# Dividing attention outputs by their row sums: normalizing after a transpose, or scaling in place with a spread copy of the reciprocals

## The chip, the core and the metric

The kernel is one program on one core of a Trainium2 chip. The core has TensorE (PE; PEld is its weight load), VectorE (DVE), ScalarE (ACT) and GpSimd (POOL), which compute, and SyncE (SP), which here only issues DMAs. Each of them works off its own instructions in a fixed order and waits at an instruction until what it needs is there; what stands behind waits too. [...] The metric is device time in microseconds (us) of one execution, lower is better.

## What is computed

Top-32 attention for 8 batches and 8 heads, 576 queries and keys, head size 64, and then a mixing layer for each batch on the 576 x 512 outputs `x`:

```
scores = q @ k.T / 8
mask = scores >= (32nd largest of the row)
attn = exp(where(mask, scores, -1e9) - rowmax)
attn = attn / (sum(attn) + 1e-9)
x = attn @ v                      # heads side by side: [batch, 576, 512]

theta = x @ w_theta
zr, zi = x * cos(theta), x * sin(theta)
u = x + w_tok_r @ zr + w_tok_i @ zi
out = u + relu(u @ w_ch)
```

The division by `sum(attn)` is linear, so the kernel does it late: `attn @ v` is computed from the raw exponentials, and each query's 64 outputs of a head are multiplied by one reciprocal afterwards. That multiplication is what is changed.

## The kernel before

**Attention.** A batch has four pairs of heads, and a pair five units: four of 128 queries for two heads, and one (j = 4) that holds the last 64 queries of both heads. A unit runs through `scores` (TensorE products, ScalarE copies half of them out), `fold` and `pick` (VectorE), `threshold` (VectorE: MAX8 and MATCH_REPLACE8, then a row on GpSimd that makes `lim`), `penalize` (ScalarE makes `pen`, GpSimd subtracts it, L304), `exponent` (ScalarE, which sums the row as it goes), `turn` (TensorE transposes to keys on partitions, ScalarE copies `at`), `mix_values` (TensorE) and `keep_values`, where ScalarE copies the result into the batch's `xt`: channels on partitions, 4 blocks of 128, and 576 queries along the row. `pipeline` interleaves these over neighbouring units: a unit's scores are written two units ahead, its exponentials one unit and its transposes two units behind. The next pair is loaded ahead (`raw`, L171), halved into `hi` (ScalarE, L189) and `raw` (GpSimd, L190), and copied into place by twelve DMAs (L202) ahead of its first scores. `raw`, `hi` and the units' `e` share nine buffers.

**Mixer.** When the last pair of a batch is kept, a generator `mixer` starts, and `advance` lets it take steps between the units that follow: ten steps in the first five units (`PLAN`), then one a unit. The batch's row sums lie with queries on partitions (`sums`), and `rinv` is their reciprocal there. In the first steps each of five blocks k of queries goes through a chain:

- four transposes of `xt` into PSUM, `px_s` (L533): queries on partitions;
- `normalize` (L434, VectorE): `px_s` times `rinv`, written to `xs`;
- `turn_back`: four transposes of `xs` into `px_t` (L449), which ScalarE copies over `xt` (L450);
- `angles` (L472, L475): `xt` times `w_theta` into `pth`;
- `fraction` (L486 ScalarE, L487 VectorE): the fractional part of the angle, into `z`.

Block 4 has 64 queries; outside the last batch its 512 channels are folded into two halves on 128 partitions. Then `trig` takes sines and cosines on ScalarE (L494 to L496) and multiplies them by `xs` on GpSimd (L497, L502). The sine needs another table than the exponential: all sines of a batch stand between two table loads, and no exponential can stand between them. Then come the token products `py` (L576), to which VectorE adds `xt` (L557), the channel products `po` (L601) and the output (L602, stored at L603).

**What sets the order.** The kernel is written as one long program. A scheduler orders each engine's instructions by priority (the place in the program, less or plus an offset: mixer steps are 100 ahead, its token and channel products 400 behind, so that these fill gaps) and by when it takes operands and buffers to be ready. Within an engine the order is then fixed. `ps_t` has two PSUM buffers for all transposes, `xs` and `z` one buffer each. The last batch (`split`) runs its products in three passes of halved numbers, with nothing of attention left beside it. A safe path that computes everything again stands behind an `If` that isn't taken.

Of the kernel before, what the change touches and what calls it, by code (L numbers as in the profile page):

```python
# [9 lines left out]
F32 = mybir.dt.float32  # L10
# [5 lines left out]
ALU = mybir.AluOpType  # L16
AX = mybir.AxisListType

P = 128
# [3 lines left out]
WEARLY = 3  # L23
AHEAD = 2
S_LATE = 0
PLAN = (2, 2, 2, 2, 2)
ORDER = "PTUFKSTVMXZ"
FOLDS = 3
M_TOK = 400
M_PE = 0  # L30
# [14 lines left out]
def topk_attention_phase_mixer(  # L45
# [11 lines left out]
    nc = tc.nc  # L57
    B, NPAIR, _, S = qT.shape
    DM = w_ch.shape[0]
    D = P // 2  # L60
    H = 2 * NPAIR
    HS = S // 2
    NJ = S // P
    REM = S - NJ * P
    NB = DM // P
    KB = 2 * NJ + 1
# [7 lines left out]
    wk2 = ctx.enter_context(tc.tile_pool(name="wk2", bufs=2))  # L74
    wk3 = ctx.enter_context(tc.tile_pool(name="wk3", bufs=3))
    one = ctx.enter_context(tc.tile_pool(name="one", bufs=1))
    ps_s = ctx.enter_context(tc.tile_pool(name="ps_s", bufs=2, space=bass.MemoryType.PSUM))
    ps_t = ctx.enter_context(tc.tile_pool(name="ps_t", bufs=2, space=bass.MemoryType.PSUM))
    ps_m = ctx.enter_context(tc.tile_pool(name="ps_m", bufs=2, space=bass.MemoryType.PSUM))

    ident = const.tile([P, P], F32, name="ident")
# [80 lines left out]
    def later(n):  # L162
        return tc.high_priority(offset=-n)
# [236 lines left out]
    def mixer(bt, split=False):  # L400
        bq, xt, sums, sums_rem = bt["bq"], bt["xt"], bt["sums"], bt["sums_rem"]
        nc.gpsimd.tensor_copy(sums[:REM, NJ, 0::2], sums_rem[0:D])
        nc.scalar.copy(sums[:REM, NJ, 1::2], sums_rem[D:P])
        rinv = wk2.tile([P, NJ + 1, H], F32, tag="rinv", name="rinv")
# [20 lines left out]
                return xs[:REM, NJ], z[:REM, 2 * NJ], last[0][:REM]  # L425
            return xs[:, NJ, :HD], last[0][:, :HD], last[0][:, HD:]

        def normalize(k, px):
            rows, parts = (P, 1) if k < NJ else (REM, folds)
            for a in range(parts):  # L430
                cols = slice(a * DM // parts, (a + 1) * DM // parts)
                out = xs[a * D : a * D + rows, k, : DM // parts]
                hs = slice(cols.start // D, cols.stop // D)
                nc.vector.tensor_tensor(  # L434
                    out.rearrange("p (h d) -> p h d", d=D),
                    px[:rows, cols].rearrange("p (h d) -> p h d", d=D),
                    rinv[:rows, k, hs].unsqueeze(2).to_broadcast([rows, hs.stop - hs.start, D]),
                    op=ALU.mult,
                )

        def turn_back(j):
            rows, parts = (P, 1) if j < NJ else (REM, folds)
            m = NB // parts
            for a in range(parts):
                sl = slice(a * D, a * D + rows)
                pt = ps_t.tile([P, NB, P], F32, tag="t", name="px_t")
                with later(M_PE):
                    for p in range(m):
                        nc.tensor.transpose(pt[:, p, :rows], xs[sl, j, p * P : p * P + P], ident[sl, sl])  # L449
                nc.scalar.copy(xt[:, a * m : a * m + m, j * P : j * P + rows], pt[:, :m, :rows])  # L450
                if split:
                    cs = slice(j * P, j * P + rows)
                    nc.scalar.copy(x_hi[:, a * m : a * m + m, cs], pt[:, :m, :rows])
                    for p in range(a * m, a * m + m, 2):
                        pp = slice(p, p + 2)
                        nc.vector.tensor_sub(x_lo[p // 2][:, :, cs], xt[:, pp, cs], x_hi[:, pp, cs].bitcast(F32))

        def angles(j):
            th[j] = ps_m.tile([P, 512], F32, tag="m", name="pth")
# [17 lines left out]
                            )  # L477

        def fraction(j):
            whole = wk2.tile([P, DM], F32, tag="whole", name="whole", bufs=1)  # L480
            if j == NJ:
                last[0] = whole
            _, zr, _ = spots(j)
            n = zr.shape[-1]
            m = zr.shape[0]
            nc.scalar.activation(whole[:m, :n], th[j][:m, :n], AF.Identity, bias=magic[:m])  # L486
            nc.vector.scalar_tensor_tensor(  # L487
                zr, whole[:m, :n], MAGIC, th[j][:m, :n], op0=ALU.subtract, op1=ALU.subtract
            )
# [28 lines left out]
        if split:  # L518
# [5 lines left out]
                z_hi.extend(flat[:, k] for k in range(flat.shape[1]))  # L524
            z_lo += two_blocks("kh", NJ, DM, "z_lo") + two_blocks("q2", NJ, DM, "z_lo")
            z_lo.append(wk2.tile([P, S], F32R, tag="lo1", name="z_lo")[:, :DM])
        for k in range(NJ + 4):
            if k <= NJ:
                rows = P if k < NJ else REM
                px = ps_t.tile([P, DM], F32, tag="t", name="px_s")  # L530
                with later(M_PE):
                    for p in range(NB):
                        nc.tensor.transpose(px[:rows, p * P : p * P + P], xt[:, p, k * P : k * P + rows], ident)  # L533
                normalize(k, px)
            if 0 <= k - 1 <= NJ:
                turn_back(k - 1)
            if 0 <= k - 3 <= NJ:
                fraction(k - 3)
            if 0 <= k - 2 <= NJ:
                angles(k - 2)  # L540
            if k < NJ + 4:
                yield
        yield
        trig(range(NJ + 1))
        yield
        late = None
# [34 lines left out]
        settle(*late)  # L581
        for m in range(NB):
            if not split:
                ot = wk2.tile([P, S], F32, tag="ot", name="ot", bufs=1)
            else:
                if m % 2 == 0:
                    ots = wk2.tile([P, 2, S], F32, tag="kh", name="ots")
                ot = ots[:, m % 2]
# [186 lines left out]
```

## Time and profile before

| | |
|---|---|
| time, median of 3 runs | 1308.51 us (1308.46 to 1309.14) |
| the profiled execution's own time | 1313.39 us |
| its span, first to last instruction | 1311.5 us |
| busy: PE, DVE, ACT, POOL | 89%, 90%, 77%, 50% of the span |
| mean granted clock of TensorE | 0.95 of full speed |

The span is one core's, so there is nothing to compare between cores. The profiled execution took 4.9 us more than the median; terms worked out from its rows are set against its own time and then taken off the median. A busy share is a mean over stretches with different limits, so the views by stretch and the chain of waits say more than the shares. Durations on GpSimd are rough, and a matmul's end is modelled.

### The profile page before, as it was taken

Reading aid. Unit: us, or ns where it says so; the run is one execution under the profiler, and the core shown is the slowest. Engines: PE = TensorE matmul, PEld = TensorE weight load, DVE = VectorE, ACT = ScalarE, POOL = GpSimd, SP = SyncE. Lnnn points to the kernel's source line nnn. Section 1 sums busy time; section 2 is a strip of 40 time slices with the busy share of each in tenths; the row PEclk is TensorE's granted clock in tenths of the full one; section 3 lists DMA queues with packets and bytes.
Section 4 is the critical chain, followed back from the end, with each engine's and each line's share of the span. In section 5 each row is a group of like instructions: output and inputs, shape, how many; then the busy total and the mean of one; then the engine's idle time right before and its main releaser. Section 6 shows DMA issues by size and latency. Waiting matters only on the chain.

```text
span 1311.5 us, 21746 instructions
## 1 busy us (share of the span) xinstructions
PE 1169.6 (89%) x6293; PEld 859.9 (66%) x6293; DVE 1181.1 (90%) x3993; ACT 1011.9 (77%) x2072; POOL 650.6 (50%) x768
## 2 busy tenths in 40 slices
PE   3666669899989998899999998899999999899998
PEld 3544445678657775577656785577756786567688
DVE  7999999899999999979999999889999999888453
ACT  4878778978788788977879878886888878786660
POOL 2445655744475445643465534553464544653640
PEclk9878769999989999999999999999998999999999
DMA  5234441433323333123323243123423144120001
GB/s 171 58 84 117 141 125 48 108 82 101 100 63 82 82 110 91 41 76 92 109 55 90 79 113 91 36 59 89 136 55 90 37 115 130 27 64 10 37 2 39
DMA packets 70720, 106.04 MB, mean 81 GB/s; under 512 B 13888, under 2 KB 32064, under 8 KB 70592
## 3 DMA queue, kind: packets, MB, share of 16 engines
q1 hardware_dynamic: 70592, 104.57, 29.5%
q8 instruction: 52, 0.85, 0.3%
q14 instruction: 76, 0.62, 0.2%
HBM read 38.40 MB, written 9.44 MB: 36 GB/s over the span
## 4 chain that ended last, share of the span: by engine, by line
PE 38%; DVE 32%; ACT 15%; issue 4%; POOL 4%; SPq 3%; DMA 3%; ACTq 0%; POOLq 0%; DVEq 0%
PE py L576 14%; DVE lst L283 9%; DVE lst L289 8%; PE pth L472 6%; PE px L357 5%; PE ps_score L234 4%; PE pt L329 3%; DVE lst L265 3%; DVE lo L266 3%; DVE lst L270 3%; SPq L202 3%; ACT e L314 3%; ACT pen L302 2%; PE po L601 2%; ACT e L243 2%
## 5 line engine op out<-in xcount | busy, mean ns | idle before, releaser
L304 POOL TENSOR_TENSOR e<-e,pen 128x576 f32<-128x576 f32 x288 | 369.1, 1299 | 208.4 <-ACT pen L302 195.4
L283 DVE MAX8 lst<-lst 128x8 f32<-128x192 f32 (+3 forms) x1152 | 423.9, 407 | 0.8
L289 DVE MATCH_REPLACE8 lst<-lst 128x192 f32<-128x192 f32 (+2 forms) x864 | 329.7, 388 | 0.0
L576 PE MATMUL py<-w,z 128*128 128x288 f32 x1008 | 272.0, 414 | 1.2 <-DMA z<-whole 1.2
L314 ACT ACTIVATE e<-e,lim 128x576 f32<-128x576 f32 x288 | 225.3, 784 | 36.4 <-POOL e L304 35.1
L234 PE MATMUL ps_score<-kh,q 128*128 128x288 f32 x512 | 188.9, 383 | 59.0 <-DVE lo L266 25.3
L302 ACT ACTIVATE pen<-e,lim 128x576 bf16<-128x576 f32 x288 | 210.7, 775 | 39.5 <-POOL lim L294 39.4
L576 PEld LDWEIGHTS py<-w,z 128*128 128x128 f32 x1008 | 185.7, 193 | 54.4 <-issue 7.1
L329 PE MATMUL pt<-ident,e 128*128 128x128 f32 x1152 | 178.6, 288 | 34.8 <-ACT e L314 21.1
L329 PEld LDWEIGHTS pt<-ident,e 128*128 128x128 f32 x1152 | 141.0, 146 | 76.4 <-ACT e L314 27.2
L357 PE MATMUL px<-at,vt 128*64 128x320 f32 (+1 forms) x1024 | 171.0, 430 | 7.7 <-ACT at L334 5.3
L243 ACT COPY e<-ps_score 128x576 f32<-128x576 f32 x256 | 162.0, 647 | 18.9 <-PE ps_score L234 14.7
L331 ACT COPY at<-pt 128x512 f32<-128x512 f32 x256 | 145.2, 587 | 28.0 <-PE pt L329 27.3
L234 PE MATMUL ps_score<-kl,q 128*128 128x288 f32 x512 | 157.5, 323 | 4.5 <-DMA kl<-raw 3.9
L234 PEld LDWEIGHTS ps_score<-kh,q 128*128 128x128 f32 x512 | 104.7, 205 | 81.9 <-ACT e L243 23.1
L265 DVE TENSOR_TENSOR lst<-ps_score,e 128x576 f32<-128x576 f32 (+1 forms) x160 | 109.6, 685 | 46.0 <-ACT e L243 20.9
L357 PEld LDWEIGHTS px<-at,vt 128*64 128x64 f32 x1024 | 78.4, 142 | 70.2 <-issue 19.5
L601 PE MATMUL po<-xt,w 128*128 128x288 f32 x448 | 119.4, 407 | 0.0
L270 DVE MAX8 lst<-lo 128x8 f32<-128x288 f32 x288 | 116.8, 441 | 0.0
L234 PEld LDWEIGHTS ps_score<-kl,q 128*128 128x128 f32 x512 | 105.8, 207 | 11.6 <-DMA kl<-raw 4.2
L472 PE MATMUL pth<-w,xt 128*128 128x512 f32 x224 | 107.4, 626 | 5.0 <-ACT xt L450 5.0
L266 DVE TENSOR_TENSOR lo<-ps_score,e 128x576 f32<-128x576 f32 (+1 forms) x160 | 109.6, 685 | 0.0
(119 smaller groups left out, 1676.5 us busy)
## 6 DMA issues: line engine op xcount, KB each, us to landing
kh<-hi SPq DMA_DIRECT2D x124, 144.0 KB, 2.7
kl<-raw SPq DMA_DIRECT2D x124, 144.0 KB, 2.6
raw<-in_qT_dram SPq DMA_DIRECT2D x31, 288.0 KB, 3.0
raw<-in_kT_dram SPq DMA_DIRECT2D x31, 288.0 KB, 3.1
q<-hi SPq DMA_DIRECT2D x62, 144.0 KB, 2.5
q<-raw SPq DMA_DIRECT2D x62, 144.0 KB, 2.6
vt<-in_v_dram SPq DMA_DIRECT2D x32, 256.0 KB, 2.9
out_dram<-ot SPq DMA_DIRECT2D x28, 288.0 KB, 2.2
```

The source lines that it names most:

```text
L234: nc.tensor.matmul(out[:, at : at + n], l, r, start=(i == 0), stop=(i == len(mm) - 1), skip_group_check=True)
L243: nc.scalar.copy(u.x[:, :, keys], u.ps[:, :, :HS])
L270: nc.vector.max(u.lst[:, w, HS:TOP], u.lo1[:, w])
L283: nc.vector.max(lst[:, w, best], part[w])
L289: nc.vector.match_replace(out=rest, in_to_replace=lst[:, w, best], in_values=part[w], imm_value=LOWEST)
L302: nc.scalar.activation(pen[:, w], u.x[:, w], AF.Relu, bias=u.lim[:, w, 0:1], scale=-STEEP)
L304: nc.gpsimd.tensor_sub(u.x[:, w], u.x[:, w], pen[:, w])
L314: nc.scalar.activation(u.x[:, w], u.x[:, w], AF.Exp, bias=u.lim[:, w, 1:2], scale=SCALE, accum_out=acc)
L329: nc.tensor.transpose(pt[:, c], e[:, w, at0 : at0 + P], ident)
L357: nc.tensor.matmul(px[sl, :n], pr["vt"][:, kb, sl], pr["at"][:, a, kb], start=(kb == 0), stop=False, skip_group_check=True)
L472: nc.tensor.matmul(th[j][: l.shape[-1]], l, r, **pos)
L576: nc.tensor.matmul(py[:, :HS], l, r, start=(i == 0), stop=(i == len(mm) - 1))
```

## The change

Outside the last batch the reciprocals go to where the channels are, instead of the channels to where the reciprocals are.

- `spread` (new): `rinv` is turned by five small transposes into `pr`, eight heads on partitions; ScalarE copies it to `row` in two pieces; one DMA writes that to `away` in device memory, and two DMAs read it back, each to 64 partitions at once, so that partition d of block p holds the 576 reciprocals of its head: `wide_r`. It takes the place of the upper half of `z`, which at that time holds nothing.
- `scale` (new): GpSimd multiplies each of the four blocks of `xt` by `wide_r` in place, 128 x 576 each.
- then, for each block of queries, `angles` on the scaled `xt`, and `turn_values`: the four transposes into `px_s`, which ScalarE copies into `xs`. `normalize` and `turn_back` are left to the last batch, for which nothing is changed.
- the steps are one for `spread`, two for `scale`, six for the blocks, one for `trig`; `PLAN` becomes (1, 2, 2, 2, 2, 2). `whole` and `ot`, with one buffer each, share two buffers with `row`.

```diff
-PLAN = (2, 2, 2, 2, 2)
+PLAN = (1, 2, 2, 2, 2, 2)
...
+    far = ctx.enter_context(tc.tile_pool(name="far", bufs=2, space=bass.MemoryType.DRAM))
...
+        def spread():
+            row = wk2.tile([P, S], F32, tag="row", name="row")[:H]
+            for js in (range(NJ), (NJ,)):
+                pr = ps_t.tile([P, NJ * P], F32, tag="t", name="pr")
+                n = 0
+                with later(M_PE):
+                    for j in js:
+                        rows = P if j < NJ else REM
+                        nc.tensor.transpose(pr[:H, n : n + rows], rinv[:rows, j], ident[:rows, :rows])
+                        n += rows
+                nc.scalar.copy(row[:, js[0] * P : js[0] * P + n], pr[:H, :n])
+            away = far.tile([NPAIR, 2, S], F32, tag="away", name="away")
+            nc.sync.dma_start(away.rearrange("p a s -> (p a) s"), row)
+            for a in range(2):
+                nc.sync.dma_start(wide_r[a * D : a * D + D], away[:, a].partition_broadcast(D))
+
+        def scale(p):
+            nc.gpsimd.tensor_mul(xt[:, p], xt[:, p], wide_r[:, p])
+
+        def turn_values(k):
...
+            px = ps_t.tile([P, DM], F32, tag="t", name="px_s")
...
+                if not split:
+                    nc.scalar.copy(out, px[:rows, cols])
+                    continue
...
+        else:
+            wide_r = z.rearrange("p k d -> p (k d)")[:, KB * DM - NB * S :].rearrange("p (b s) -> p b s", s=S)
+            spread()
+            yield
+            for p in range(NB):
+                scale(p)
+                if p % 2:
+                    yield
+            for k in range(NJ + 2):
+                if k <= NJ:
+                    angles(k)
+                    turn_values(k)
+                if k:
+                    fraction(k - 1)
+                yield
         trig(range(NJ + 1))
```

The order on TensorE at the start of the fifth mixer, before. `px` with 320 columns is the last product of the batch's attention, `ps_score` are scores of the units that follow.

```order
L357 MATMUL px_8151<-at1_8003,vt_7440 64x320 x8
L360 MATMUL px_8151<-rem1_8004,vrem1_94 128x320
L329 MATMUL pt_8212<-ident_76,e_7939 128x128 x4
L533 MATMUL px_s_8253<-ident_76,xt_6804 128x128 x4
L234 MATMUL ps_score_8421<-kh_8173,q2_8172 128x288
...
L533 MATMUL px_s_8259<-ident_76,xt_6804 128x128 x4
L449 MATMUL px_t_8265<-ident_76,xs_8251 128x128 x4
...
L472 MATMUL pth_8352<-w_121,xt_6804 128x512
```

And after the change:

```order
L358 MATMUL px_8097<-at1_7949,vt_7386 64x320 x8
L361 MATMUL px_8097<-rem1_7950,vrem1_96 128x320
L440 MATMUL pr_8200<-ident_78,rinv_8192 8x128 x4
L440 MATMUL pr_8206<-ident_78,rinv_8192 8x64
L235 MATMUL ps_score_8324<-kh_8119,q2_8118 128x288
...
L496 MATMUL pth_8342<-w_123,xt_6727 128x512
L456 MATMUL px_s_8347<-ident_78,xt_6727 128x128
...
L496 MATMUL pth_8353<-w_123,xt_6727 128x512
L456 MATMUL px_s_8358<-ident_78,xt_6727 128x128
```

The small transposes take the place of the first `px_s`; the first angles stand 20 score products behind them instead of 16 behind the first `px_s`, and interleave with the transposes of the same blocks, and `px_t` is gone. Counted through the whole order, a batch has 168 score products (8.4 a unit). In mixers three to six, 50 of them (50 in each) stand between the first `px_s` and the first token product before, 108 to 110 between that and the last channel product, and 8 to 10 from there to the next mixer. After the change, from the first `pr` on, these are 62, 100 and 6. In the first mixer they are 42, 112 and 16 before, and 42, 127 and 7 after. On ScalarE 46 to 48 instructions stand from the sine's table load to the exponential's before, 41 after: two `pen`, two `at` and one `whole` fewer.

The order on GpSimd at the same place, before; the unit of `e_8223` (j = 4 of the next batch's first pair) is the same in both, and `raw` belongs to that batch's second pair:

```order
L294 TENSOR_TENSOR lim_8393<-lst_8236,factors_90 128x2
L304 TENSOR_TENSOR e_8223<-e_8223,pen_8478 128x576
L190 TENSOR_TENSOR raw_8550<-raw_8550,hi_8650 128x1152
L502 TENSOR_TENSOR z_8252<-xs_8251,z_8252 128x512
L296 COPY marks_87<-lst_8322 128x10
L497 TENSOR_TENSOR z_8252<-xs_8251,z_8252 128x512
```

And after the change:

```order
L295 TENSOR_TENSOR lim_8302<-lst_8182,factors_92 128x2
L305 TENSOR_TENSOR e_8169<-e_8169,pen_8375 128x576
L449 TENSOR_TENSOR xt_6727<-xt_6727,z_8198 128x576 x4
L297 COPY marks_89<-lst_8264 128x10
L191 TENSOR_TENSOR raw_8460<-raw_8460,hi_8553 128x1152
L295 TENSOR_TENSOR lim_8378<-lst_8264,factors_92 128x4
```

All four multiplications stand in a row, ahead of the next pair's `raw` and of the next `lim`; the first product with a sine (L502 before, L526 after) stands nine rows behind that unit's `e` instead of two. The order on SP at the same place, before:

```order
L603 DMA out_0_dram<-ot_7970 128x576
L206 DMA vt_8190<-in_v_dram 128x4x128
L209 DMA vrem1_94<-in_v_dram 64x64 x2
L171 DMA raw_8550<-in_qT_dram 128x576
L171 DMA raw_8550<-in_kT_dram 128x576
```

And after the change:

```order
L637 DMA out_0_dram<-ot_7916 128x576
L207 DMA vt_8136<-in_v_dram 128x4x128
L210 DMA vrem1_96<-in_v_dram 64x64 x2
L444 DMA away_8209<-row_8199 8x576
L446 DMA z_8198<-away_8209 64x4x576 x2
L172 DMA raw_8460<-in_qT_dram 128x576
L172 DMA raw_8460<-in_kT_dram 128x576
```

The write, and the two reads that wait for it, now stand ahead of the next pair's loads.

## Rows read from the trace of the kernel before

**Rows 1.** Page, part 1: busy us (share of the span) x instructions, each engine.

```profile
PE 1169.6 (89%) x6293; PEld 859.9 (66%) x6293; DVE 1181.1 (90%) x3993; ACT 1011.9 (77%) x2072; POOL 650.6 (50%) x768
```

**Rows 2.** Windows: seven front stretches; columns us, busy of PE, PEld, DVE, ACT, POOL.

```profile
794.50:839.50 45.00, 39.33 (x194) 23.77 (x192) 42.44 (x146) 34.05 (x67) 24.66 (x28) 0.96 0.23 60
...
sum 317.20, PE 277.80 PEld 169.62 DVE 307.31 ACT 257.80 POOL 185.22; mean PE 39.69 PEld 24.23 DVE 43.90 ACT 36.83 POOL 26.46
```

**Rows 3.** Windows: seven product stretches, first token product to last channel product.

```profile
839.50:939.50 100.00, 97.14 (x541) 74.56 (x541) 88.30 (x311) 78.25 (x167) 45.25 (x57) 1.00 0.35 92
...
sum 698.70, PE 680.84 PEld 524.71 DVE 630.89 ACT 555.97 POOL 340.30; mean PE 97.26 PEld 74.96 DVE 90.13 ACT 79.42 POOL 48.61
```

**Rows 4.** Windows: a stretch between mixers; last three columns clock, DMA share, GB/s.

```profile
335.30:341.80 6.50, 6.43 (x47) 4.74 (x46) 6.50 (x22) 5.33 (x14) 3.59 (x3) 1.00 0.94 245
```

**Rows 5.** Chain that ended last, 780 to 960 us: start, us, engine and line.

```profile
819.12 5.14 PE pth L472 x8
...
828.19 3.63 PE pth L472 x8
...
842.56 1.28 ACT L314
843.86 4.66 ACT e L314 x12
...
854.88 4.56 PE py L576 x18
...
901.63 0.76 DVE lst L265
```

**Rows 6.** Groups by form: xcount | busy us, mean ns | idle before and releasers.

```profile
L304 POOL TENSOR_TENSOR e<-e,pen 128x576 f32<-128x576 f32 x288 | 369.1, 1299 | 208.4 <-ACT pen L302 195.4 <-issue 8.7 <-DMA wraw<-in_w_tok_i_dram 2.6
L302 ACT ACTIVATE pen<-e,lim 128x576 bf16<-128x576 f32 x288 | 210.7, 775 | 39.5 <-POOL lim L294 39.4
L472 PE MATMUL pth<-w,xt 128*128 128x512 f32 x224 | 107.4, 626 | 5.0 <-ACT xt L450 5.0
L449 PE MATMUL px_t<-ident,xs 128*128 128x128 f32 x128 | 21.6, 294 | 8.7 <-DVE xs L434 5.6 <-ACT at L331 2.4 <-ACT x_hi L453 0.8
L487 DVE SCALAR_TENSOR_TENSOR z<-whole,pth 128x512 f32<-128x512 f32 x32 | 21.6, 674 | 9.2 <-ACT whole L486 9.2
L434 DVE TENSOR_TENSOR xs<-px_s,rinv 128x512 f32<-128x512 f32 x32 | 21.4, 670 | 3.5 <-PE px_s L533 3.5
L533 PE MATMUL px_s<-ident,xt 128*128 128x128 f32 x128 | 21.0, 291 | 2.3 <-ACT at L331 2.3
L450 ACT COPY xt<-px_t 128x512 f32<-128x512 f32 x32 | 18.7, 584 | 8.9 <-PE px_t L449 8.6
L434 DVE TENSOR_TENSOR xs<-px_s,rinv 64x256 f32<-64x256 f32 x14 | 5.8, 412 | 0.1
```

**Rows 7.** DMA issues: xcount, KB each, median us to landing.

```profile
kh<-hi SPq DMA_DIRECT2D x124, 144.0 KB, 2.7
raw<-in_kT_dram SPq DMA_DIRECT2D x31, 288.0 KB, 3.1
out_dram<-ot SPq DMA_DIRECT2D x28, 288.0 KB, 2.2
```

**Rows 8.** Timelines of SP, ACT, POOL and PE, fifth mixer: start, us, what, [idle].

```profile
794.72 0.43 ACT L369 COPY xt<-px 128x320 f32<-128x320 f32 x1
796.07 0.44 SPq L171 DMA_DIRECT2D raw<-in_kT_dram  x1
804.15 2.64 POOL L190 TENSOR_TENSOR raw<-raw,hi 128x1152 fp32r<-128x1152 f32 x1 [0.57 <-ACT hi L189]
811.50 1.28 ACT L494 ACT_TABLE_LOAD   x1
811.79 1.24 SPq L202 DMA_DIRECT2D kl<-raw  x2
818.25 0.40 PE L234 MATMUL ps_score<-kh,q 128*128 128x288 f32 x1 [2.33 <-DVE lo L266]
```

More of the change, by code (lines that the diff above doesn't have):

```diff
@@ L426, in spots @@
             return xs[:, NJ, :HD], last[0][:, :HD], last[0][:, HD:]
-        def normalize(k, px):
+        def spread():
[16 more added lines that the diff above has]
+        def turn_values(k):
             rows, parts = (P, 1) if k < NJ else (REM, folds)
+            px = ps_t.tile([P, DM], F32, tag="t", name="px_s")
+            with later(M_PE):
+                for p in range(NB):
+                    nc.tensor.transpose(px[:rows, p * P : p * P + P], xt[:, p, k * P : k * P + rows], ident)
             for a in range(parts):
@@ L432, in normalize @@
                 out = xs[a * D : a * D + rows, k, : DM // parts]
+                if not split:
+                    nc.scalar.copy(out, px[:rows, cols])
+                    continue
                 hs = slice(cols.start // D, cols.stop // D)
-                nc.vector.tensor_tensor(
+                nc.vector.tensor_mul(
                     out.rearrange("p (h d) -> p h d", d=D),
@@ L437, in normalize @@
                     rinv[:rows, k, hs].unsqueeze(2).to_broadcast([rows, hs.stop - hs.start, D]),
-                    op=ALU.mult,
                 )
         def turn_back(j):
[L442 to L456, printed above, removed]
+            rows = P if j < NJ else REM
+            cs = slice(j * P, j * P + rows)
+            pt = ps_t.tile([P, NB, P], F32, tag="t", name="px_t")
+            for p in range(NB):
+                nc.tensor.transpose(pt[:, p, :rows], xs[:rows, j, p * P : p * P + P], ident[:rows, :rows])
+            nc.scalar.copy(xt[:, :, cs], pt[:, :, :rows])
+            nc.scalar.copy(x_hi[:, :, cs], pt[:, :, :rows])
+            for p in range(0, NB, 2):
+                pp = slice(p, p + 2)
+                nc.vector.tensor_sub(x_lo[p // 2][:, :, cs], xt[:, pp, cs], x_hi[:, pp, cs].bitcast(F32))
         def angles(j):
@@ L479, in fraction @@
         def fraction(j):
-            whole = wk2.tile([P, DM], F32, tag="whole", name="whole", bufs=1)
+            whole = wk2.tile([P, S], F32, tag="row", name="whole")[:, :DM]
             if j == NJ:
@@ L526, in mixer @@
             z_lo.append(wk2.tile([P, S], F32R, tag="lo1", name="z_lo")[:, :DM])
[L527 to L541, printed above, removed]
-                yield
-        yield
+        if split:
+            for k in range(NJ + 4):
+                if k <= NJ:
+                    turn_values(k)
+                if 0 <= k - 1 <= NJ:
+                    turn_back(k - 1)
+                if 0 <= k - 3 <= NJ:
+                    fraction(k - 3)
+                if 0 <= k - 2 <= NJ:
+                    angles(k - 2)
+                yield
+            yield
[3 more added lines that the diff above has]
+            yield
+            for p in range(NB):
+                scale(p)
+                if p % 2:
+                    yield
+            for k in range(NJ + 2):
+                if k <= NJ:
+                    angles(k)
+                    turn_values(k)
+                if k:
+                    fraction(k - 1)
+                yield
         trig(range(NJ + 1))
@@ L583, in mixer @@
             if not split:
-                ot = wk2.tile([P, S], F32, tag="ot", name="ot", bufs=1)
+                ot = wk2.tile([P, S], F32, tag="row", name="ot")
             else:
```

## The prediction

> **What bounds the kernel now.** The page first: TensorE is busy for 89% of the span and VectorE for 90% [rows 1]. So neither can simply be "the" limit, and I cut the span by what the mixer does. The windows give three kinds of stretch in each batch. In the front stretch, from the first transpose of a mixer to its first token product, VectorE is busy for 43.9 of 45.3 us on average (317.2 / 7) and TensorE for 39.7 [rows 2]: VectorE is the limit. In the product stretch, to the last channel product, TensorE is busy for 97.3 of 99.8 us (698.7 / 7) and VectorE for 90.1 [rows 3]: TensorE is the limit. In the few us between mixers VectorE is never idle [rows 4]. The chain of waits shows where one limit takes over from the other. From 819 to 832 us it runs through the angles on TensorE, then to 843 through the sines on ScalarE (which end with the table load), the exponentials that had to wait for them (twelve pieces at once from 843.86), then the token products from 855 to about 900, and from 901.6 VectorE again [rows 5]. So a microsecond saved on VectorE counts in the front and just before it, and not in the middle of the products.
>
> **What goes.** VectorE loses `normalize`: per batch 4 x 0.670 + 2 x 0.412 = 3.5 us [rows 6], all of it in the front stretch, where VectorE is the limit. For seven batches 24.5 us; that is the most that this term alone can give. TensorE loses the second transposes, 21.6 / 8 = 2.7 us per batch and a little for block 4 [rows 6], in the same stretch; there it had 5 us to spare, so I count nothing for it. The wait of the angles for `turn_back` (5.0 us in all, behind L450) goes too, on the same spare engine.
>
> **What is added.** ScalarE copies `px_s` out instead of `px_t`: the same count and size (0.584 us each [rows 6]), so nothing, apart from two small copies of eight partitions, well under 1.2 us together; ScalarE has 45.3 - 36.8 = 8.5 us free in the stretch [rows 2]. The five small transposes replace twenty. GpSimd gets four multiplications of 128 x 576; the subtraction of the same shape took 1.299 us [rows 6], so 5.2 us per batch in one piece. GpSimd is busy for 26.5 of 45.3 us there [rows 2], so the sum is covered; its place in the queue is not free, and is priced below.
>
> **What moves.** The angles need the scaled `xt`, and so come about one unit later. The order shows how far: before, 50 score products, 109 and 9 in the three stretches (5.95, 12.98 and 1.07 units); after, 62, 100 and 6 (7.38, 11.90 and 0.71). So 1.43 units enter the front, 1.07 leave the product stretch and 0.36 the gap. What a unit costs depends on who is the limit. On VectorE: 43.9 less normalize 3.5 and fraction 3.1 (4 x 0.674, and 0.41 as its half-width twin in normalize), over 5.95 units: 6.3 us. In the product stretch it saves at least what it costs TensorE: 39.7 less angles 15.3 (107.4 / 7), and 2.6 and 2.7 for the two transposes [rows 6], over 5.95: 3.2 us. It saves at most a whole unit's time there, 99.8 / 12.98 = 7.7 us. So per batch:
>
> front +1.43 x 6.3 - 3.5 = +5.5; gap -0.36 x 6.3 = -2.3; products -1.07 x (3.2 to 7.7) = -3.4 to -8.2. Sum: -0.2 to -5.0 us.
>
> The chain is on TensorE for the first half of the product stretch and on VectorE for the second [rows 5], so I take the middle, -2.6. For the second to seventh batch that is -15.6 us. The first mixer's angles don't move in the order (42 products before and after); it gets the -3.5 alone. Together -19.1 us.
>
> **The new wait.** The DMAs are no longer only loads ahead of need: the write, two reads, four multiplications and the next pair's preparation form one row. SP issues the write after ScalarE's copy, waits until it has landed (0.4 and 2.2 us, as the output's store [rows 7]), and only then issues the reads, 0.6 us each; behind them stand the next pair's loads. The reads move 2 x 64 x 4 x 2304 bytes = 1.18 MB. The busiest stretch shown moved 245 GB/s at a DMA share of 0.94 [rows 4], so 261 when full: 4.5 us, and about 2 us for the first bytes (a transfer of half the size of another took 2.7 us against 3.1 [rows 7], so most of a small one is fixed). The reciprocals are thus in place 9.1 us after the copy. That copy stands right behind the last `xt` copy, at 794.72 to 795.2 us in the fifth mixer [rows 8]; say 796. GpSimd then scales from 805.1 to 810.3, and takes `raw` at 810.3 instead of 804.15 [rows 8], 6.2 us late. The loads themselves, 3.8 us late in issue and queued behind 3.3 us of reads, land 7.1 us later than at 799.2 (796.07 + 3.1), at 806.3, in time for that. What slack is there? The last of the pair's copies was issued at 812.4 and landed 2.7 us later, at 815.1; the first score that needs the pair began at 818.25, and TensorE had waited there 2.33 us for VectorE [rows 8]. So 3.1 us of the 6.2 are covered by slack that the trace shows, and up to 3.1 us per batch can show on TensorE. The bounds are 0 and 3.1. I take 0.6, nearer to 0, since only the last of twelve copies is that late and TensorE was ahead of VectorE there. It makes +4.2 us for seven batches.
>
> [...]
>
> **Sum.** -19.1 + 4.2 = -14.9 us. The profiled execution would go from 1313.4 to 1298.5, and the median from 1308.5 to 1293.6: I forecast 1294 us, from 1284 to 1304.
>
> **Rivals.**
>
> *The shift eats the saving.* If TensorE stays the limit through the whole product stretch, a unit taken out of it saves 3.2 us, and the same unit costs 6.3 in the front. For it: TensorE is busy for 97.5% there [rows 3]. Against it: VectorE carries the chain from 901.6 us on [rows 5]. Then -0.2 x 6 - 3.5 + 4.2 = -0.5: 1308 us, with a range of 1304 to 1311.
>
> *The pair comes late (slower).* The wait above is paid in full and VectorE starves behind it: 3.1 us plus whatever the reads take above 4.5, six times. The saving of 19.1 is used up at 3.2 us per batch, that is when the reads take 4.6 us; at 5.0 us the kernel is slower by more than 0.2%. At 6 us it is 6 x 4.6 - 19.1 = +8.5: 1317 us, between 1311 and 1326. For it: GpSimd works strictly in order, and `raw` and the next `lim` stand behind the multiplications. Against it: all that is queued behind must be late at once, and TensorE was waiting for VectorE at the critical place.
>
> *The sines get shorter.* The exponentials stand still from 811.5 to 843.9 us [rows 5, 8], and the chain runs through that. Five ScalarE instructions leave this stretch: two `pen` of 0.775 us (L302), and three copies at about 0.6, as L450 [rows 6]: 3.4 us. The waits for the later angles (819 to 824 and 828 to 832 us in the chain) can go too, as the first two blocks' angles are done sooner. If the 3.4 count in six batches, 20 us come on top: 1274 us, between 1268 and 1284. For it: the chain. Against it: the instructions are moved out, not removed.
>
> **How the numbers follow.** Forecast 0.43, shift 0.17, late pair 0.22, shorter sines 0.18. A measurement of this kernel can tell about 0.2%, 2.6 us, from no change: 1305.9 to 1311.1. Of the shift 0.05 lies below that and 0.12 within. Faster: 0.43 + 0.18 + 0.05 = 0.66; same: 0.12; slower: 0.22. The range from 1276 to 1318 leaves out about half of the shorter sines and a quarter of the late pair, 0.15 together.
>
> **What the profile after would show.** VectorE busy for about 3.5 us less per batch in all, and still over 95% in the front stretch, which is now about 50 us long; the product stretch 94 to 97 us. GpSimd idle for 1 to 2 us ahead of the multiplications, waiting for a DMA. `pth` waiting for GpSimd little or not at all, since 20 score products stand ahead of it. The next pair's first scores waiting for a DMA by 1 us or less. The prediction is wrong if the front is not bound by VectorE after the change, if the reads land later than 10 us after the copy, or if VectorE's waits for `lim` (GpSimd) grow by more than 1 us per batch.

## The result and the profile after

The changed kernel takes 1317.68 us (median of 5 runs, 1316.12 to 1322.29) against 1308.51 us for the kernel before (median of 5 runs, 1308.46 to 1310.11): ratio 1.0076, 95% interval 1.0053 to 1.0098. It is slower by 0.8%, where 1294 us were forecast; 1317 us was the price of the rival called "the pair comes late". The profiled execution took 1322.29 us, with a span of 1320.5 us (before 1313.39 and 1311.5).

Part 1 of the page after the change, to be read against [rows 1]: by these totals VectorE shed 18.8 us of work and TensorE 16.6, and GpSimd took on 37.6. Yet the span grew, so both wait more than before.

```profile
PE 1153.0 (87%) x6188; PEld 855.7 (65%) x6188; DVE 1162.3 (88%) x3951; ACT 1013.3 (77%) x2086; POOL 688.2 (52%) x796
```

The windows of the front stretches after the change, from the first small transpose to the first token product (fifth mixer, and the sum over seven; us, then busy time of PE, PEld, DVE, ACT, POOL, then granted clock, DMA share, GB/s):

```profile
805.50:859.60 54.10, 44.87 (x213) 28.71 (x212) 47.29 (x168) 41.30 (x83) 33.87 (x37) 0.87 0.35 88
...
sum 367.80, PE 301.77 PEld 194.94 DVE 329.77 ACT 290.54 POOL 236.43; mean PE 43.11 PEld 27.85 DVE 47.11 ACT 41.51 POOL 33.78
```

And the sum line of the product stretches after the change:

```profile
sum 667.40, PE 648.26 PEld 501.83 DVE 597.21 ACT 531.59 POOL 329.96; mean PE 92.61 PEld 71.69 DVE 85.32 ACT 75.94 POOL 47.14
```

Against [rows 2] the front went from 45.3 to 52.5 us, and VectorE from 97% to 90% of it: it is no longer the limit there. Against [rows 3] the product stretch went from 99.8 to 95.3 us. The front took 50.6 us more in all, the products gave 31.3 back, and the few us between mixers and the end 10.3.

What the front waits for stands in the chain of waits after the change, fifth mixer (start, us, what):

```profile
807.95 0.56 ACT row L442 x2
808.53 1.50 DMA away<-row
810.04 0.61 SPq L446
810.70 8.29 DMA z<-away
819.12 1.41 POOL xt L449
820.57 2.08 PE pth L496 x2
...
838.35 1.28 ACT L518
...
861.28 1.28 ACT L315
```

Before, the chain had no transfer at this place. From the end of ScalarE's copy (808.51) to the first multiplication it is 10.6 us; 9.1 were estimated, with 6.5 for the reads, which took 8.3. In the list of waits after the change (engine and line, waited for: us in total, times, longest) three did not exist before (`pth` behind `xt`, `xt` behind `z`, `hi` behind `raw`), and three were shorter:

```profile
ACT pen L303 <- POOL lim L295: 72.1, 46, 9.2
...
DVE lst L266 <- POOL lim L295: 31.4, 14, 5.9
...
PE pth L496 <- POOL xt L449: 28.6, 6, 6.6
POOL xt L449 <- DMA z<-away: 27.5, 6, 5.0
...
DVE z L511 <- ACT whole L510: 20.9, 14, 2.9
...
ACT hi L190 <- DMA raw<-in_kT_dram: 14.0, 5, 3.1
```

Before, the wait of `pen` was 39.4 us and that of `z` 9.2 [rows 6], and VectorE's wait for `lim` was

```profile
DVE lst L265 <- POOL lim L294: 18.9, 10, 4.4
```

TensorE's timeline shows what the 20 score products ahead of the angles were worth as cover. They were through by 814.9; two products with the values and one group of transposes follow, and then TensorE stands still for 4.8 us:

```profile
814.62 0.29 PE L235 MATMUL ps_score<-kl,q 128*128 128x288 f32 x1
814.76 0.59 PE L361 MATMUL px<-rem,vrem 128*128 128x256 f32 x2
815.19 0.60 PE L330 MATMUL pt<-ident,e 128*128 128x128 f32 x4
820.57 2.08 PE L496 MATMUL pth<-w,xt 128*128 128x512 f32 x2 [4.78 <-POOL xt L449]
```

### The profile page after: what moved, and what is told of

Its sections match the earlier page's. It is cut to its first block, busy times and chain, and to the rows that moved or that the text cites. A ratio compares the mean times of both kernels' runs of the same rounds, so it can differ in the third digit from the quotient of the medians.

```text
span 1320.5 us, 21625 instructions
## 1 busy us (share of the span) xinstructions
PE 1153.0 (87%) x6188; PEld 855.7 (65%) x6188; DVE 1162.3 (88%) x3951; ACT 1013.3 (77%) x2086; POOL 688.2 (52%) x796
## 4 chain that ended last, share of the span: by engine, by line
PE 33%; DVE 28%; ACT 22%; DMA 7%; issue 4%; POOL 3%; SPq 3%; ACTq 0%; DVEq 0%; POOLq 0%
PE py L610 13%; DVE lst L284 8%; DVE lst L290 8%; PE pth L496 5%; ACT e L315 4%; PE ps_score L235 4%; PE px L358 4%; DMA z<-away 4%; ACT pen L303 4%; PE pt L330 3%; DVE lo L267 3%; PE po L635 3%; ACT e L244 3%; DVE lst L266 2%; DVE lst L271 2%
## 5 line engine op out<-in xcount | busy, mean ns | idle before, releaser
L284 DVE MAX8 lst<-lst 128x8 f32<-128x192 f32 (+3 forms) x1152 | 418.6, 407 | 0.7
L610 PE MATMUL py<-w,z 128*128 128x288 f32 x1008 | 275.1, 414 | 1.8 <-DVE whole L511 1.1
L303 ACT ACTIVATE pen<-e,lim 128x576 bf16<-128x576 f32 x288 | 209.3, 771 | 72.4 <-POOL lim L295 72.1
L330 PE MATMUL pt<-ident,e 128*128 128x128 f32 x1152 | 185.8, 291 | 23.4 <-ACT e L315 22.2
L330 PEld LDWEIGHTS pt<-ident,e 128*128 128x128 f32 x1152 | 146.0, 148 | 64.5 <-ACT e L315 33.4
L266 DVE TENSOR_TENSOR lst<-ps_score,e 128x576 f32<-128x576 f32 (+1 forms) x160 | 109.7, 686 | 71.9 <-POOL lim L295 31.4
L235 PE MATMUL ps_score<-kl,q 128*128 128x288 f32 x512 | 163.8, 335 | 5.1 <-DMA kl<-raw 4.6
L235 PEld LDWEIGHTS ps_score<-kh,q 128*128 128x128 f32 x512 | 106.3, 209 | 93.5 <-issue 29.7
L358 PE MATMUL px<-at,vt 128*64 128x320 f32 (+1 forms) x1024 | 160.8, 429 | 4.9 <-ACT at L335 3.5
L496 PE MATMUL pth<-w,xt 128*128 128x512 f32 x224 | 117.2, 646 | 28.6 <-POOL xt L449 28.6
L235 PEld LDWEIGHTS ps_score<-kl,q 128*128 128x128 f32 x512 | 107.6, 212 | 12.9 <-issue 5.4
```

The source lines that it names most:

```text
L235: nc.tensor.matmul(out[:, at : at + n], l, r, start=(i == 0), stop=(i == len(mm) - 1), skip_group_check=True)
L284: nc.vector.max(lst[:, w, best], part[w])
L303: nc.scalar.activation(pen[:, w], u.x[:, w], AF.Relu, bias=u.lim[:, w, 0:1], scale=-STEEP)
L330: nc.tensor.transpose(pt[:, c], e[:, w, at0 : at0 + P], ident)
L358: nc.tensor.matmul(px[sl, :n], pr["vt"][:, kb, sl], pr["at"][:, a, kb], start=(kb == 0), stop=False, skip_group_check=True)
L496: nc.tensor.matmul(th[j][: l.shape[-1]], l, r, **pos)
```

## The experiments

Theories. **Wait:** the trip through memory stands between the last values and the first angles, and its length is paid. **Shift, order:** the angles' and sines' later place in the order costs, whatever delivers the reciprocals. **GpSimd queue:** the four multiplications in one piece hold up `lim` and `raw`. **Traffic:** the reads hold up the next pair's loads. All times, with the ratio to the kernel before on the same chip (its medians there lay between 1306.1 and 1309.7 us); e1, e5 and e11 leave the normalization out:

| run | us | ratio (95%) |
|---|---|---|
| e1 no trip | 1287.08 | 0.984 (0.981 to 0.987) |
| e2 before, one unit later | 1352.16 | 1.035 (1.033 to 1.037) |
| e3 multiplied by query blocks | 1321.90 | 1.010 (1.006 to 1.013) |
| e4 trip ahead | 1320.60 | 1.011 (1.008 to 1.014) |
| e5 trip unused | 1289.65 | 0.987 (0.983 to 0.991) |
| e6 reads twice | 1358.62 | 1.038 (1.035 to 1.042) |
| e7 spread by TensorE | 1346.85 | 1.030 (1.027 to 1.033) |
| e8 and multiplied by VectorE | 1347.29 | 1.030 (1.028 to 1.033) |
| e9 trip ahead, by pairs | 1357.86 | 1.038 (1.036 to 1.041) |
| e10 the same, half a unit later | 1368.72 | 1.048 (1.046 to 1.050) |
| e11 no trip, order held | 1282.08 | 0.980 (0.976 to 0.983) |
| e12 trip, order of e1 held | 1355.88 | 1.037 (1.033 to 1.040) |
| e13 trip ahead, order held | 1289.13 | 0.986 (0.984 to 0.988) |
| e14 trip a little ahead, order held | 1295.16 | 0.990 (0.988 to 0.992) |

**e1, e5: without the trip, and with a trip that nobody waits for.**

```diff
-            away = far.tile([NPAIR, 2, S], F32, tag="away", name="away")
-            nc.sync.dma_start(away.rearrange("p a s -> (p a) s"), row)
-            for a in range(2):
-                nc.sync.dma_start(wide_r[a * D : a * D + D], away[:, a].partition_broadcast(D))
...
-            nc.gpsimd.tensor_mul(xt[:, p], xt[:, p], wide_r[:, p])
+            nc.gpsimd.tensor_mul(xt[:, p], xt[:, p], half_pi.to_broadcast([P, S]))
```

e5 makes the last of these edits alone and keeps the four other lines.

> Of the changed kernel the write to memory and the two reads back are left out, and GpSimd multiplies by a constant column instead of the reciprocals, so the values are not normalized; everything else stays, the five small transposes and their copies too. Theory 'wait' (the loss is the wait for the round trip: GpSimd idle for 27.5 us behind the reads in six mixers, the angles 28.6 us behind GpSimd): 1288 to 1300 us. Theory 'shift' (the angles come a unit later whatever delivers the reciprocals): 1308 to 1318 us. Theory 'GpSimd queue' (four multiplications in one piece hold up the next lim and raw): 1308 to 1318 us as well.

> As the run without a round trip (1287 us; GpSimd multiplies by a constant column, so the values are not normalized), but the write and the two reads are issued as in the changed kernel and land in the same place; nothing waits for them but the later overwriting of that place. The order on TensorE is the same as in that run. Theory 'wait' (the time until the reciprocals are in place holds up the first angles): 1285 to 1291 us. Theory 'traffic' (1.18 MB of reads in each mixer hold up the loads and copies of the next pair, behind which the scores wait): 1300 to 1318 us.

1287 and 1290 us: e5 lies in the range of "wait", e1 0.9 us below it. Both have the same order on TensorE, so the transfers by themselves cost 2.6 us, less than their intervals can tell apart: "traffic" falls. GpSimd's four multiplications still stand in one piece: "GpSimd queue" falls as the main cause, as long as nothing makes GpSimd wait in front of them. But in e1 the scheduler had also put the angles 8 to 12 score products behind the small transposes, instead of 20 to 24, so order was not excluded.

**e2: the kernel before, one unit later.**

```diff
-PLAN = (2, 2, 2, 2, 2)
+PLAN = (0, 2, 2, 2, 2, 2)
```

> The kernel before with one edit: PLAN = (0, 2, 2, 2, 2, 2), so that every step of a mixer comes one unit later; normalize, turn_back and the rest as before. Theory 'shift': if the later angles cost what the change lost against its saving (9.2 + 18.8 us of VectorE work saved = 28), this kernel is slower by 15 to 28 us: 1324 to 1336 us. Theories 'wait' and 'GpSimd queue': the later place alone costs little, 1308 to 1314 us.

46 us more than the kernel before on that chip, above even the bound for "shift". So a place in the order can cost that much in this kernel, and every later run that lets the order move is open to this doubt. Why one unit costs so much was not taken apart.

**e3: multiplications cut by query blocks.**

```diff
-            nc.gpsimd.tensor_mul(xt[:, p], xt[:, p], wide_r[:, p])
+            cs = slice(k * P, min(k * P + P, S))
+            nc.gpsimd.tensor_mul(xt[:, :, cs], xt[:, :, cs], wide_r[:, :, cs])
```

> The changed kernel with the scaling cut the other way: five multiplications by block of queries (4 x 128 columns, the last 4 x 64) instead of four by block of channels, each issued just ahead of the angles that need it. The reads stay as they are. Theory 'GpSimd queue': lim waits at most 1.3 us instead of up to 5.5 behind the multiplications, the 72.1 us of pen behind lim fall back towards 39.4: 1300 to 1308 us. Theory 'wait': the first angles need one multiplication instead of four, but still the reads: 4 us of the 4.8 per mixer behind GpSimd go, if nothing else is late then 1300 to 1312. Theory 'shift': 1314 to 1319 us.

No gain, and all three theories missed, "wait" too, by 10 us. `pen` waited only 30.0 us for `lim` (72.1 after the change), so that wait is not what costs; GpSimd still waited 21.7 us for the reads, TensorE 18.2 for the multiplications and VectorE 21.8 for `lim`. The order moved here as well: 16 to 32 score products stand ahead of the angles from the second mixer on.

**e6: the wait made longer.**

```diff
-            for a in range(2):
-                nc.sync.dma_start(wide_r[a * D : a * D + D], away[:, a].partition_broadcast(D))
+            for _ in range(2):
+                for a in range(2):
+                    nc.sync.dma_start(wide_r[a * D : a * D + D], away[:, a].partition_broadcast(D))
```

> The changed kernel with both reads issued twice into the same place, so that the second pair waits for the first: about 8 us more until the reciprocals are in place, in seven mixers. Theory 'wait': 6 to 8 us more in six or seven mixers, 1350 to 1375 us. Theory 'shift' (it is the place of the angles in the order that costs): 1316 to 1325 us, unless the place moves too. Theory 'GpSimd queue' (the multiplications, not the reads, are what stands in the way): 1316 to 1325 us.

41 us more, as "wait" had it. But the order moved here too: only 50 to 54 score products stand in the front stretch from the fourth mixer on (62 after the change), and TensorE waits 18.0 us for the multiplications, less than after the change.

**e7, e8: the trip replaced by TensorE.** A selection of zeros and ones (8 x 128) times the row of reciprocals gives the same spread rows in PSUM.

```diff
-            nc.sync.dma_start(away.rearrange("p a s -> (p a) s"), row)
+                    nc.tensor.matmul(pw, pick8[:, 2 * p : 2 * p + 2].rearrange("p h d -> p (h d)"), row[:, : NJ * P], start=True, stop=True)
+                nc.scalar.copy(wide_r[:, p, : NJ * P], pw)
```

e8 has no copies to `wide_r`: VectorE multiplies `xt` by `pw`.

> The changed kernel without the write and the reads: the eight rows of reciprocals are spread over the channels' partitions by TensorE (per mixer four products of 512 and four of 64 columns with a selection of zeros and ones, some 3 us) and copied into the same place by ScalarE (five copies, some 3 us). GpSimd's four multiplications and all behind them stay. Theory 'wait': the trip of 10.5 us becomes about 5 us of work that takes no memory, 1287 to 1302 us. Theory 'GpSimd queue' or 'shift': 1312 to 1322 us.

> As the run with TensorE's spreading, but VectorE multiplies, straight from the accumulator (per mixer four pieces of 512 columns at about 0.67 us and four of 64), so that GpSimd has nothing of it and ScalarE no copies; VectorE gets back about 3.5 us per mixer. Theory 'GpSimd queue': faster than the run with GpSimd's multiplications by 5 us or more. Theory 'wait' with VectorE bound in the front: slower than it by 5 to 24 us.

Both missed every range that I had set; e7 missed "wait" as I had put it since the replacement was no shorter. In e7's fifth mixer the row was ready at 820.31, and GpSimd began at 831.11, 10.8 us later:

```profile
821.83 7.19 PE L448 MATMUL pw<-row,xs 8*128 8x512 f32 x8
828.82 1.80 PE L453 MATMUL pw<-row,xs 8*128 8x64 f32 x8
```

```profile
831.11 5.53 POOL L457 TENSOR_TENSOR xt<-xt,z 128x576 f32<-128x576 f32 x4 [5.12 <-ACT z L454]
```

Nine us of products where I had estimated three. These two runs therefore don't decide between the theories; that e8 is no faster, with nothing of it on GpSimd, speaks once more against the GpSimd queue.

**e4, e9, e10: the trip started ahead.** In e4 it is issued behind the last exponentials of the batch; in e9 and e10 in three parts, as the pairs finish, with each block multiplied as soon as it is copied.

```diff
+            if old and old.j == NJ and old.p == NPAIR - 1 and old.bq < B - 1:
+                with later(M_REST):
+                    prepare(old.batch)
```

> The changed kernel with the reciprocals, the small transposes, the copy, the write and the reads issued about two units ahead of the mixer, right behind the last exponentials of the batch; the multiplications, the angles and PLAN stay where they are. Theory 'wait': GpSimd's 27.5 us behind the reads vanish, 1288 to 1300 us. Theories 'shift' and 'GpSimd queue': 1312 to 1318 us, since the angles and the four multiplications keep their places.

> The changed kernel with the trip made ahead of need: the reciprocals of the first two pairs' four heads, then those of the third, then of the fourth pair are turned, written and read back right behind the last exponentials of these pairs, and GpSimd multiplies each block of xt right after its last columns are copied; only the last pair's trip (an eighth to a quarter of the bytes each) can stand in the way, and its block is complete two units after its exponentials. The reciprocals lie in the memory of xs instead of z's. PLAN = (2, 2, 2, 2): blocks from the mixer's first step. Theory 'wait': GpSimd's 27.5 us behind the reads go below 5, the front from first angles or transposes to first token product is 40 to 46 us, and the time 1275 to 1295 us. If the time stays over 1305 with that wait gone, 'wait' is wrong.

> The same with PLAN = (1, 2, 2, 2, 2, 2), so that the blocks start half a unit later and the sines come a little later. Theory 'wait': within 10 us of the run with (2, 2, 2, 2), since the reciprocals are in place for both. Theory 'shift' (the place of angles and sines in the order): slower than it by 10 to 25 us.

None fits "wait". e4 lies 2.6 us above what "shift" and "GpSimd queue" had, and e10 is 10.9 us slower than e9, just within what "shift" had. In e4 the trip did move ahead, but so did the multiplications: GpSimd went to them at 804.6 and stood there for 6.6 us, with the next `lim` behind it; over six mixers it waited 27.8 us, as long as after the change. TensorE's wait for the multiplications fell to 7.5 us, but VectorE's for `lim` stayed at 30.4.

```profile
811.11 4.11 POOL L456 TENSOR_TENSOR xt<-xt,z 128x576 f32<-128x576 f32 x3 [6.55 <-DMA z<-away]
815.17 0.20 POOL L295 TENSOR_TENSOR lim<-lst,factors 128x4 f32<-128x4 f32 x1
```

In e9 the whole order moved, GpSimd still waited 29.7 us for the reads (36.5 in e10), and ScalarE's `xt` copies waited 80.5 us for `px` (18.2 after the change). Which part of that makes e9 40 us slower than the changed kernel stays open. What all three share with e1 and e2 is that the order was free.

**e11, e12: the order held.** The issue order of one kernel was recorded and added to another as edges that order the issue on an engine and wait for nothing.

```diff
+            for d in steps:
+                k += d
+                if prev is not None:
+                    tc.add_manual_dep(
+                        mine[k],
+                        prev.name,
+                        mybir.DependencyInfo(mybir.DependencyClass.NoSync, mybir.DependencyReason.DATA),
+                        reason="replay",
+                    )
+                prev = mine[k]
```

> The run without a round trip (write and reads left out, GpSimd multiplies by a constant column, so the values are not normalized), but with every instruction of TensorE, ScalarE, VectorE and GpSimd held in the order that the changed kernel has (a recorded list, added as issue-order edges). It differs from the changed kernel by the trip alone. Theory 'wait': 1287 to 1300 us, as without the held order. Theory 'order' (the run without a trip gained since its angles stand 8 to 12 score products behind the small transposes instead of 20 to 24): 1310 to 1318 us.

> The changed kernel, with the trip, but TensorE, ScalarE and VectorE held in the order of the run without a trip (angles 8 to 12 score products behind the small transposes). Theory 'wait': the same 10.5 us until the reciprocals are in place, with fewer scores to pass them: 1318 to 1335 us. Theory 'order': 1288 to 1305 us.

e11 differs from the changed kernel by the trip and by the constant that it multiplies by, and takes 35.6 us less (1317.68 to 1282.08; against the kernel before a ratio of 0.980). That is 5 us below the range of "wait"; "order" falls as the cause of the loss. Its front stretches, and the sum over its product stretches:

```profile
780.00:824.70 44.70, 39.74 (x213) 25.81 (x212) 44.70 (x158) 40.20 (x82) 31.94 (x37) 1.00 0.29 80
...
sum 326.70, PE 283.40 PEld 181.88 DVE 324.15 ACT 287.37 POOL 228.15; mean PE 40.49 PEld 25.98 DVE 46.31 ACT 41.05 POOL 32.59
```

```profile
sum 666.00, PE 645.64 PEld 501.46 DVE 603.18 ACT 534.46 POOL 331.44; mean PE 92.23 PEld 71.64 DVE 86.17 ACT 76.35 POOL 47.35
```

The products are as after the change (666.0 and 667.4); 41.1 of the 45.1 us by which the two traces differ lie in the front, 46.7 us instead of 52.5, and there VectorE is busy for 99% again. VectorE's wait for `lim` is 9.5 us (31.4 after the change), that of `z` for `whole` 5.4 (20.9):

```profile
DVE lst L314 <- POOL lim L343: 9.5, 8, 1.6
...
DVE z L555 <- ACT whole L554: 5.4, 4, 2.9
```

e12 shows the other half: the trip in an order that leaves less time for it is worse still, 21 us above the range of "wait" and far from that of "order", with TensorE waiting 56.6 us for the multiplications.

```profile
PE pth L572 <- POOL xt L525: 56.6, 7, 9.6
```

**e13, e14: the order held, the trip ahead.** The marked steps (reciprocals, small transposes, copies, write, reads) are left out of the held order and issued earlier, in the fifth mixer, measured against the last copy of `xt`, the small transposes 12 us ahead in e13 and 6 in e14, the reads 9.6 and 6.5; everything else, the multiplications too, keeps the place that it has after the change.

```diff
-            row = wk2.tile([P, S], F32, tag="row", name="row")[:H]
...
+        row = z.rearrange("p k d -> p (k d)")[:H, :S]
...
+                and i.name not in moved
```

> The changed kernel with every instruction held in the order it has there, but for the reciprocals, their small transposes and copies, the write and the reads: these are issued right behind the last exponentials of the batch, some 8 score products (10 to 17 us) ahead of their old place, and the row lies in z's free lower half. The output is the full one. Theory 'wait': the 10.5 us of the trip pass while the last values are still being summed; GpSimd's 27.5 us behind the reads go below 8 and the time comes close to the run without a trip in the same order (1282 us): 1280 to 1294 us. Theory 'traffic or small steps' (the transposes, copies and reads cost by being there, wherever they are): 1305 to 1318 us.

> The same, but issued only one unit ahead of the old place, some 6 score products or 4 to 6 us. Theory 'wait': about half of the trip stays in front, and the time lies between, 1288 to 1306 us. Theory 'traffic or small steps': 1305 to 1318 us.

1289 and 1295 us: both are faster than the kernel before and the changed one, with the full output. In e13's fifth mixer the reads are issued at 788.2, and GpSimd comes to the multiplications at 801.3 without a wait:

```profile
786.08 0.30 SPq L477 DMA_DIRECT2D away<-z  x1
...
788.21 1.28 SPq L479 DMA_DIRECT2D z<-away  x2
```

```profile
800.08 1.29 POOL L352 TENSOR_TENSOR e<-e,pen 128x576 f32<-128x576 f32 x1 [2.47 <-ACT pen L350]
801.32 5.54 POOL L510 TENSOR_TENSOR xt<-xt,z 128x576 f32<-128x576 f32 x4
```

From the last copy of `xt` to the first angle it takes, in each of mixers three to seven, 7.7 us in e11, 7.2 in e13 and e14, 12.0 to 12.6 after the change and 21.8 to 23.2 in e6. In e13 VectorE's wait for `lim` is down as in e11, and TensorE's for the multiplications to 3.1 us (28.6 after the change), while `pen` waits for `lim` nearly as long as after the change (72.1), so that wait isn't what costs:

```profile
ACT pen L350 <- POOL lim L342: 69.7, 42, 5.0
...
DVE lst L313 <- POOL lim L342: 9.3, 8, 1.7
```

Over the seven mixers the first angles of e13 come 29.0 us earlier than after the change, in sum (the first 1.7 later, the others 4.8 to 5.5 earlier), and 28.6 were measured. e11 is 7.1 us below e13; its four multiplications by a constant take 4.46 us, against 5.54 with `wide_r`, and seven times the difference is 7.6, so the trip itself may cost nothing more there. In e14 GpSimd doesn't wait for the reads either: no half of the trip is left in front, and that its time lies in the range of "wait" shows nothing of that half. Why it is 6 us above e13, with the same 7.2, was not pursued; one wait differs by as much, that of the transposes for ScalarE's copies of the row (7.7 us in e14, 1.6 in e13), but that it is the cause isn't shown.

## Why the prediction was wrong

**What bounds the kernel** was read rightly, and e11 shows that it would have stayed so: VectorE 99% of the front, TensorE 97% of the products. The changed kernel left this state: VectorE at 90% of the front. The prediction had named three signs of being wrong, and all three came: the front is not bound by VectorE, the reads landed 10.5 us after the copy (more than 10), and VectorE's wait for `lim` grew from 18.9 to 31.4 us, 1.8 per batch (more than 1).

**What goes** was right: 3.5 us of VectorE per batch were forecast, and the rows of `normalize` fell from 27.9 to 3.4 us, those of the last batch, which is 3.5 in each of seven. VectorE's total fell by 18.8 us only, since other instructions took longer in this execution, most of all the preparation of the weights at the start (43.0 us before, 46.4 after).

**What moves** was mis-sized, but not to the bad side. Forecast per mixer: front +5.5, products -3.4 to -8.2, between mixers -2.3. With the trip taken out (e11) the front is 46.7 us against 45.3, so +1.4, and the products 95.1 against 99.8, so -4.7; the rest of the span lost 12.9 us in all, where 6 x 2.3 = 13.8 were forecast. (These are the traced executions, which lie 36.1 us apart; the medians lie 27.6 apart.) So it is the front's term that was wrong: 1.43 more units, with normalize gone, raised VectorE's busy time there from 43.9 to 46.3 us, not by 5.5. The sum without the wait, -19.1 us, stands against -27.6 in e11 and -19.0 in e13; with a front term 4 us per mixer too high, that e13 meets it is partly luck. The rival "the shift eats the saving" is wrong by this; e2 shows only that another shift, of another kernel, is dear.

**The new wait** is the step that failed. What was priced was GpSimd coming late to the next pair's `raw`; the waits of the angles and of `lim` behind the same multiplications were put at nothing. The whole was put between 0 and 3.1 us per batch and taken as 0.6, or 4.2 us in all. It costs 28.6 us (against e13) to 35.6 (against e11, which saves on the multiplications as well), 4 to 5 us per mixer, more than the upper bound. It reached the front by two ways. GpSimd stands in front of the multiplications, and with it the next `lim`, for which VectorE waits (31.4 us, 9.3 in e13); and the angles come late, and with them `whole` and `z` (20.9 us, 5.0 in e13). So VectorE, the limit of the front, stands idle there for 38.0 us (367.8 - 329.8) instead of 2.6 in e11 (326.7 - 324.2). How much each way costs by itself isn't shown. Two errors made this:
- The bound was worked out for the wrong one of those who wait. I followed the next pair's loads and copies, found 3.1 us of slack for them, left `lim` to a rival, and settled the angles in half a sentence: 20 score products stand ahead. These were through 6.4 us after the row's copy; the trip and the first multiplication took 12.1. A count of instructions ahead is no cover until it is turned into us.
- The trip was put too short: it took 10.6 us instead of 9.1 (the write and the issue of the first read 2.1, where 2.6 were put for the write alone; the reads 8.3 instead of 6.5), with GpSimd idle for 4.6 us per mixer (27.5 / 6) where 1 to 2 were forecast. The rate came from the busiest stretch shown [rows 4], with other transfers in it; why the reads ran longer isn't shown.

**The rival that gave the time**, "the pair comes late", had its price right (6 x 4.6 = 27.6 us for the wait, against 28.6), and a part of its mechanism: VectorE does starve, and `lim` behind the multiplications is one of the two ways. The other, the angles, is missing from it, and the pair that gives it its name shows as 14.0 us of ScalarE waiting for `raw` only; so that the price meets the time to 1 us is in part luck. The forecast's own range ended at 1304; the wider one, to 1318, reaches the time only by this rival's share in it. "The sines get shorter" did happen: from the table load to the exponentials' the fifth mixer has 838.35 to 861.28 on ScalarE after the change, 23 us, against 811.50 to 842.56, 31 us, before [rows 5, 8]. The fifth mixer of e11 has 21.3. That can be a part of what e11 gains beyond the forecast, 27.6 against 19.1 us, but no run isolates it, and it is not the 20 us on top that the rival had.

## What to carry to other kernels

Where a value is sent through memory between two engines, price the trip from the last producer to the first consumer in us, and the cover in us as well: what stands ahead in the consumer's queue, and how long it runs. Price it for everyone who waits, also for what stands in the queue of the engine that stands still. Start such a trip when its data are ready, not where its result is needed; here the reciprocals of the fifth mixer were ready 22 us before their transposes (783.5 and 805.5 us), and moving the trip alone, with everything else held in its order, turned a loss of 9 us into a gain of 19. In a kernel whose order is made by a scheduler, hold the order fixed to learn what one step costs: runs that let it move answered with 46 us (e2) or 40 (e9) of something else.

## What the runs showed of the hardware

In the fifth mixer TensorE also ran slower behind this wait. After its 4.8 us of idleness the first two angle products took 2.08 us, and the same two took 1.02 in e13; the granted clock over 815.8 to 826.4 us was 0.68, and 1.00 in e13 around its first angles (801 to 808 us):

```profile
815.80:826.40 10.60, 5.83 (x12) 3.04 (x13) 8.88 (x32) 3.06 (x5) 7.28 (x6) 0.68 0.66 163
```

```profile
801.00:808.00 7.00, 7.00 (x37) 4.83 (x36) 7.00 (x26) 4.78 (x9) 7.00 (x7) 1.00 0.18 42
```

```profile
802.93 1.02 PE L557 MATMUL pth<-w,xt 128*128 128x512 f32 x2
```

The 213 matrix products of the fifth front take 44.9 us of TensorE's busy time after the change, at a granted clock of 0.87, and 39.7 in e11, at 1.00. That the idleness is what lowered the clock is not shown. Over the whole span the granted clock was 0.936 after the change, 0.950 before, 0.954 in e13.

A low clock was granted in e7 too. TensorE had stood still for 1.62 us, to 819.82:

```profile
819.82 0.40 PE L235 MATMUL ps_score<-kh,q 128*128 128x288 f32 x1 [1.62 <-ACT e L244]
```

Then, by its records, it was busy without a gap from 820.1 to 833.8 us, and the granted clock over these 13.7 us was 0.50; what ran there were scores, the products with 8 rows, and transposes (the ends of matrix products are modelled in such records, so a gap between them can be hidden). Why it was so low is not shown.

```profile
820.10:833.80 13.70, 13.70 (x38) 8.71 (x37) 13.70 (x54) 6.41 (x15) 4.17 (x4) 0.50 0.01 3
```
